# Sixty-four more bytes behind each buffer of a rotating operand: where the tiles lie in SBUF

## The chip, the cores and the metric

The kernel runs on one core of one Trainium2 chip, in one launch. The metric is the device time of that core in microseconds. Before the change three runs took 1132.81, 1133.07 and 1133.88 us, a median of 1133.07 us.

## The reference

Three layers follow each other on 6016 tokens of 256 channels, all in float32.

```
qn, kn = q, k divided by their norms over the tokens          # 6016 x 256 each
a      = softmax(kn.T @ qn / tau)                             # 256 x 256
x      = v @ a                                                # 6016 x 256
h      = relu(x @ w_in)                                       # 6016 x 2048
x      = (h * h) @ w_out                                      # 6016 x 256
xn     = x / sqrt(mean(x * x) + 1e-6) * rms_g
out    = (silu(xn @ w_gate) * (xn @ w_val)) @ w2              # inner width 1536
```

## The kernel before, in words

**Precision.** A float32 product is made from three products of a faster 4-byte type (fp32r). Each operand is split in a high part, a rounded copy, and a low part, the value less the high part. `mm3` (L102 to L105) then issues high by high (L103), high weight by low data (L104) and low weight by high data (L105) into one PSUM bank. Every matmul has 128 rows, 128 columns of weights and up to 512 columns of data, and every one has its own weight load.

**Stages.** The attention part (L449 to L640) runs over q and k once, up to about 62 us. Then the first MLP runs over twelve blocks of tokens, ten of 512 and two of 448 (`mlp1`, L741): for each of 16 slices of the 2048 inner channels `up` issues two `mm3` into one bank, so 6 matmuls, the ScalarE takes relu out of it (tile r, in `o6` or `o7`), the square s goes to `o8` or `o9`, its high part to `sh` (L761 or L764, ScalarE) and its low part to `sl` (L768, VectorE), and `down` (L772) issues 6 matmuls that read `sh` and `sl` into two accumulators. From about 596 us the second MLP (`mlp2`, L959) runs over six pairs of blocks and twelve slices of its inner channels: 21 matmuls at L984 make two blocks' gate and value by seven products of sums and differences; the product of silu and value is split into `sh` (L1047, ScalarE) and `sl` (L1051, VectorE), and again `down` reads both with 12 matmuls, six for each block.

**Order.** The order of the work is written out by hand: `unit` (L704) issues one slice's `up`, its reads, the side work hooked to it and an older slice's `down`. No scheduler or planner looks at an address.

**Tiles.** A pool gives each tag its own place in every partition of SBUF, in the order of the tags' first use, one behind the other. The pool `xp` holds, in this order, `o4`, `o5`, `o10` to `o13`, `o7`, `o9`, five buffers of `sh`, five of `sl`, `o6`, `o8`, two buffers of `ys` (4,096 bytes each; also the split inputs of block 2 and of the second MLP on their way to DRAM, and `x4`), and `xst` (14,336 bytes; in the odd pairs it holds as `xs` three of the second MLP's seven inputs). Behind it lies the small pool `ns`. All other tags are in pools ahead of these. The five `sh` and five `sl` buffers are handed out in turn by `work` (L731):

```
    def work(tag, n):
        return xp.tile([P, NB], F32R, tag=tag, name=tag, bufs=5)[:, :n]
```

NB is 512, so a buffer takes 2,048 bytes of each partition. Every tag in the list is a multiple of 512 bytes long, and each of them starts at 128 mod 512. So does every slice that a matmul of the two MLPs reads, weights too, since those are slices of 128 or 256 four-byte columns.

Of the kernel before, what the change touches and what calls it, by code (L numbers as in the profile page):

```python
# [9 lines left out]
F32R = mybir.dt.float32r  # L10
# [8 lines left out]
P = 128  # L19
NB = 512  # L20
WARM = 8
SIGN = -(2**31)


@with_exitstack
def attn_moe_kernel(ctx: ExitStack, tc, q, k, v, tau, w_in, w_out, w_gate, w_val, w2, rms_g, out):
# [88 lines left out]
    class Call:  # L115
# [27 lines left out]
        def b2(self):  # L143
            gi = self.g.bitcast(I32)
            nc.vector.scalar_tensor_tensor(
                out=gi, in0=self.raw[:, 1::2], scalar=SIGN, in1=gi, op0=ALU.bitwise_and, op1=ALU.bitwise_or
            )
# [301 lines left out]
    with tc.tile_pool(name="qk", bufs=3) as qp:  # L449
# [55 lines left out]
        def warm(count):  # L505
            for _ in range(count):
                nc.tensor.matmul(nk, busy[:, :P], busy, start=True, stop=True)
# [10 lines left out]

        warm(WARM)
        for ci, (j0, nj) in enumerate(chunks):  # L520
# [124 lines left out]
    xp = ctx.enter_context(tc.tile_pool(name="xp", bufs=1, reuse_waits="tile"))  # L645
# [83 lines left out]
            pending.pop(0)()  # L729

    def work(tag, n):  # L731
        return xp.tile([P, NB], F32R, tag=tag, name=tag, bufs=5)[:, :n]

    turns = {"r": 0, "s": 0}

# [5 lines left out]
    def mlp1(b, vt, act_heavy):  # L741
# [4 lines left out]
        def up(f):  # L746
            o = mm()[:, :n]
            fs = slice(f * P, (f + 1) * P)
            for c in range(KC):
                mm3(o, m_h[:, c, fs], m_l[:, c, fs], vt["h"][c], vt["l"][c], c == 0, c == KC - 1)  # L750

            def read(evs):
                r, s = turn("r", n), turn("s", n)
                sh, sl = work("sh", n), work("sl", n)
                sq[f] = sh, sl, s
                nc.scalar.activation(out=r, in_=o, func=AF.Relu)  # L756
                for x in evs:
                    x()
                if act_heavy(f):
                    nc.scalar.activation(out=s, in_=r, func=AF.Square)  # L760
                    nc.scalar.copy(out=sh, in_=s)  # L761
                else:
                    nc.vector.tensor_tensor(out=s, in0=r, in1=r, op=ALU.mult)
                    nc.scalar.activation(out=sh, in_=r, func=AF.Square)  # L764

            def rest():
                sh, sl, s = sq[f]
                nc.vector.tensor_tensor(out=sl, in0=s, in1=f32(sh), op=ALU.subtract)  # L768

            return read, rest  # L770
# [188 lines left out]
    def mlp2(p, ops, after_product, after_group, spare):  # L959
# [17 lines left out]
        def group(f):  # L977
# [67 lines left out]
            def hi(t, x):  # L1045
                parts[t] = work("sh", n), work("sl", n)
                nc.scalar.copy(out=parts[t][0], in_=x)  # L1047
# [181 lines left out]
    n, last_mean = norm_steps(NBLK - 1, ys[NBLK - 1])  # L1229
# [87 lines left out]
```

## Time and profile before

| what | value |
|---|---|
| median of three runs | 1133.07 us |
| profiled execution, from first to last instruction | 1130.9 us |
| TensorE matmul busy | 1118.5 us, 99% |
| ScalarE busy | 764.7 us, 68% |
| VectorE busy | 748.5 us, 66% |
| DMA, mean over the span | 89 GB/s |

The page gives no device time of its own for the profiled execution beside its span. The span is 2.2 us shorter than the median of the runs, and these 2.2 us lie around it, before the first and after the last instruction. A matmul's busy time counts from its start until its modelled end, and matmuls overlap, so 99% busy says that TensorE is hardly ever without a matmul, not how fast they follow each other. For that one reads the distance from one start to the next.

### The profile page before, as it was taken

To read this page: it belongs to the slowest core of one execution; us is meant where nothing else is said; L and a number is where in the kernel's file an instruction comes from. 1 tells how busy PE (TensorE), PEld (TensorE's weight loads), DVE (VectorE), ACT (ScalarE), POOL (GpSimd) and SP (SyncE) were. 2 spreads that over 40 slices of the span, in tenths; PEclk is the share of its full clock that TensorE was granted. 3 is DMA by queue.
4 is the path that set the end of the run, shared out by engine and by line. 5 is a ranking of instruction groups with operands and counts; after the bars stand their busy time and mean duration, and the time that the engine had idled before them with its cause. 6 is when DMAs were issued, how large, how long until landed. Compare 5 with 4: busy or idle time off the path is not lost.

```text
span 1130.9 us, 14479 instructions
## 1 busy us (share of the span) xinstructions
PE 1118.5 (99%) x5222; PEld 943.0 (83%) x5222; DVE 748.5 (66%) x1156; ACT 764.7 (68%) x1382; POOL 72.9 (6%) x99
## 2 busy tenths in 40 slices
PE   8999999999999999999999999999999999999997
PEld 7978888888888888889987888888888888888996
DVE  6998766687777787766556655555655655655655
ACT  7688867677687787776677566556656566556554
POOL 2421110010202020100000000000000000000000
PEclk9999999999999999999999999999999999999999
DMA  9733310231451532320247023202302302202001
GB/s 318 232 112 94 94 38 20 84 121 38 130 159 66 156 139 68 110 101 1 85 149 313 33 103 104 74 1 75 94 1 75 93 1 75 71 16 66 19 19 33
DMA packets 96903, 101.21 MB, mean 89 GB/s; under 512 B 49856, under 2 KB 67520, under 8 KB 96320
## 3 DMA queue, kind: packets, MB, share of 16 engines
q1 hardware_dynamic: 94560, 99.44, 27.7%
q10 hardware_dynamic: 2272, 0.85, 0.3%
q8 instruction: 41, 0.67, 0.3%
q14 instruction: 30, 0.25, 0.1%
HBM read 65.21 MB, written 35.06 MB: 89 GB/s over the span
## 4 chain that ended last, share of the span: by engine, by line
PE 92%; DMA 2%; ACT 2%; DVE 1%; POOL 1%; issue 1%; SPq 1%; DVEq 0%; ACTq 0%
PE mm L984 29%; PE acc L103 13%; PE acc L104 13%; PE acc L105 13%; PE mm L105 7%; PE mm L104 7%; PE mm L103 7%; POOL rows L492 1%; DMA rraw<-in_v_dram 1%; PE mm L683 1%; DMA qraw<-in_k_dram 1%; ACT hl L532 0%; DMA o<-xd 0%; SPq L461 0%; SPq L462 0%
## 5 line engine op out<-in xcount | busy, mean ns | idle before, releaser
L984 PE MATMUL mm<-o,gv 128*128 128x512 f32 (+1 forms) x1152 | 294.5, 387 | 0.7 <-DMA o<-xd 0.6
L984 PEld LDWEIGHTS mm<-o,gv 128*128 128x128 f32 x1152 | 214.9, 188 | 45.6 <-ACT pu L1029 1.1
L768 DVE TENSOR_TENSOR sl<-o,sh 128x512 fp32r<-128x512 f32 (+1 forms) x192 | 134.4, 700 | 104.4 <-ACT sh L761 89.9
L1051 DVE TENSOR_TENSOR sl<-hp,sh 128x512 fp32r<-128x512 f32 (+1 forms) x144 | 98.0, 681 | 143.1 <-ACT sh L1047 142.7
L1012 ACT COPY mm<-mm 128x512 f32<-128x512 f32 (+1 forms) x72 | 40.4, 561 | 183.9 <-PE mm L984 183.9
L756 ACT ACTIVATE o<-mm 128x512 f32<-128x512 f32 (+1 forms) x192 | 112.3, 585 | 69.3 <-PE mm L105 65.8
L103 PE MATMUL acc<-sh,wo_h 128*128 128x512 f32 (+1 forms) x384 | 149.0, 388 | 0.0
L105 PE MATMUL mm<-o,m_l 128*128 128x512 f32 (+1 forms) x384 | 148.2, 386 | 0.4 <-DVE m_l L695 0.4
L105 PE MATMUL acc<-sh,wo_l 128*128 128x512 f32 (+1 forms) x384 | 148.1, 386 | 0.1
L104 PE MATMUL acc<-sl,wo_h 128*128 128x512 f32 (+1 forms) x384 | 148.1, 386 | 0.0
L103 PE MATMUL mm<-o,m_h 128*128 128x512 f32 (+1 forms) x384 | 147.9, 385 | 0.0
L104 PE MATMUL mm<-o,m_h 128*128 128x512 f32 (+1 forms) x384 | 147.9, 385 | 0.0
L103 PE MATMUL acc<-sh,w_h 128*128 128x512 f32 (+1 forms) x284 | 109.5, 386 | 0.0
L105 PE MATMUL acc<-sh,w_l 128*128 128x512 f32 (+1 forms) x284 | 109.5, 385 | 0.0
L104 PE MATMUL acc<-sl,w_h 128*128 128x512 f32 (+1 forms) x284 | 109.5, 385 | 0.0
L1047 ACT CAST sh<-hp 128x512 fp32r<-128x512 f32 (+1 forms) x144 | 89.0, 618 | 2.7 <-DVE hp L1038 1.9
L105 PEld LDWEIGHTS mm<-o,m_l 128*128 128x128 f32 x384 | 72.1, 188 | 14.8 <-DVE m_l L695 1.5
L105 PEld LDWEIGHTS acc<-sh,wo_l 128*128 128x128 f32 x384 | 72.1, 188 | 14.3 <-DVE wo_l L170 0.8
L104 PEld LDWEIGHTS mm<-o,m_h 128*128 128x128 f32 x384 | 72.1, 188 | 13.5
L103 PEld LDWEIGHTS mm<-o,m_h 128*128 128x128 f32 x384 | 72.1, 188 | 13.4
L104 PEld LDWEIGHTS acc<-sl,wo_h 128*128 128x128 f32 x384 | 72.1, 188 | 13.3 <-DVE sl L768 0.4
L103 PEld LDWEIGHTS acc<-sh,wo_h 128*128 128x128 f32 x384 | 72.1, 188 | 13.0 <-ACT wo_h L163 0.2
(153 smaller groups left out, 1767.6 us busy)
## 6 DMA issues: line engine op xcount, KB each, us to landing
xd<-xp SPq DMA_DIRECT2D x70, 256.0 KB, 2.1
o<-xd SPq DMA_DIRECT2D x56, 256.0 KB, 4.6
raw<-in_moe_w_out_dram SPq DMA_DIRECT2D x14, 512.0 KB, 3.7
gv<-gvd SPq DMA_DIRECT2D x4, 1792.0 KB, 14.0
gvd<-gp SPq DMA_DIRECT2D x12, 512.0 KB, 3.2
out_dram<-ot SPq DMA_DIRECT2D x40, 128.0 KB, 2.5
qraw<-in_q_dram SPq DMA_DIRECT2D x13, 384.0 KB, 8.0
qraw<-in_k_dram SPq DMA_DIRECT2D x13, 384.0 KB, 8.1
```

Source lines behind the costliest of these rows:

```text
L103: nc.tensor.matmul(o, wh, xh, start=start, stop=False)
L104: nc.tensor.matmul(o, wh, xl, start=False, stop=False)
L105: nc.tensor.matmul(o, wl, xh, start=False, stop=stop)
L492: nc.gpsimd.tensor_copy(out=rows[:, g], in_=src[:, g])
L683: nc.tensor.matmul(o[m], a_part(t, c, m), w[:, c], start=ts is not last and i == 0, stop=ts is not early and i == len(ts) - 1,)
L756: nc.scalar.activation(out=r, in_=o, func=AF.Relu)
L768: nc.vector.tensor_tensor(out=sl, in0=s, in1=f32(sh), op=ALU.subtract)
L984: nc.tensor.matmul(bank, c[:, hl, a, fs], x, start=start and j == 0, stop=j == 2, skip_group_check=not start)
L1012: cp(out=bu, in_=b0)
L1047: nc.scalar.copy(out=parts[t][0], in_=x)
L1051: dve(out=pl, in0=x, in1=f32(ph), op=ALU.subtract)
```

## The change

The five `sh` buffers are 2,112 bytes apart instead of 2,048. Only their first 512 columns (or 448) are used, as before; the 64 bytes behind them are never read or written.

```
+PAD = 16
     def work(tag, n):
-        return xp.tile([P, NB], F32R, tag=tag, name=tag, bufs=5)[:, :n]
+        width = NB + PAD if tag == "sh" else NB
+        return xp.tile([P, width], F32R, tag=tag, name=tag, bufs=5)[:, :n]
```

The built program has the same instructions on every engine, in the same order and with the same waits. What differs is the addresses (bytes in a partition, and the remainder by 512):

| tiles | before | after |
|---|---|---|
| pools ahead of `xp`; `o4`, `o5`, `o7`, `o9` to `o13` | 128 | 128 |
| `sh`, five buffers | 181,376 and so on, all 128 | 181,376 and so on: 128, 192, 256, 320, 384 |
| `sl`, five buffers | 191,616 and so on, 128 | 191,936 and so on, 448 |
| `o6`, `o8` | 128 | 448 |
| `ys`, two buffers (also `o2` of block 2, `xp`, `x4`) | 128 | 448 |
| `xst`, `xs` | 214,144, 128 | 214,464, 448 |
| `ns`, two buffers of 128 bytes | 128, 256 | 448, 64 |

The tiles of the attention part (`qraw`, `hl`, `rraw`, `ws`, `ws2`) and the buffers of the output (`vraw`, `vt`) stay where they are.

## Rows read from the trace of the kernel before

**Rows 1.** Busy time of each engine, and the granted clock in 40 slices.

```profile
PE 1118.5 (99%) x5222; PEld 943.0 (83%) x5222; DVE 748.5 (66%) x1156; ACT 764.7 (68%) x1382; POOL 72.9 (6%) x99
PEclk9999999999999999999999999999999999999999
```

**Rows 2.** Windows: busy time and (count) of PE, PEld, DVE, ACT, POOL; clock, DMA.

```profile
0.00:70.00 70.00, 65.59 (x468) 59.15 (x469) 57.30 (x78) 51.62 (x73) 22.51 (x44) 0.98 0.78 244
70.00:600.00 530.00, 529.01 (x2410) 444.93 (x2409) 383.26 (x610) 398.81 (x711) 50.38 (x55) 1.00 0.30 96
600.00:1100.00 500.00, 499.94 (x2231) 417.46 (x2231) 292.21 (x444) 301.10 (x573) 0.00 (x0) 1.00 0.20 64
1100.00:1131.00 31.00, 23.99 (x117) 21.44 (x115) 15.70 (x27) 13.21 (x27) 0.00 (x0) 0.94 0.14 30
```

**Rows 3.** Waits of TensorE's matmuls after 70 us: total us, times, longest.

```profile
PE mm L984 <- DMA o<-xd: 0.6, 1, 0.6
PE mm L105 <- DVE m_l L695: 0.4, 1, 0.4
```

**Rows 4.** Chain of waits, 625 to 632 us: start, length, what.

```profile
625.57 2.72 PE mm L984 x12
628.29 0.23 PE acc L103
628.52 0.23 PE acc L104
628.75 0.23 PE acc L105
628.97 1.36 PE mm L984 x6
```

**Rows 5.** Timeline of TensorE in the attention part: start, length, operation.

```profile
25.89 0.28 PE L566 MATMUL acc<-hl 128*128 128x256 f32 x1
...
26.49 0.28 PE L568 MATMUL acc<-hl 128*128 128x256 f32 x1
```

**Rows 6.** Three short windows, columns as in rows 2.

```profile
8.20:9.10 0.90, 0.90 (x6) 0.90 (x6) 0.51 (x1) 0.36 (x1) 0.00 (x0) 0.50 1.08 370
25.80:26.70 0.90, 0.90 (x10) 0.90 (x9) 0.80 (x2) 0.86 (x2) 0.00 (x0) 1.00 1.10 349
625.00:632.00 7.00, 7.00 (x33) 5.79 (x32) 5.55 (x9) 3.95 (x8) 0.00 (x0) 1.00 0.01 2
```

**Rows 7.** Timeline of TensorE in a block of 448 columns.

```profile
559.73 0.36 PE L104 MATMUL acc<-sl,wo_h 128*128 128x448 f32 x1
...
565.60 0.37 PE L103 MATMUL mm<-o,m_h 128*128 128x448 f32 x1
```

**Rows 8.** Tile `sh`: who writes and reads it; ns min/median/max, first and last start.

```profile
L103 PE MATMUL acc<-sh,wo_h x384: 362/389/476, 68.4 to 595.0; 128*128 128x512 f32 x160, 128*128 128x448 f32 x32
L105 PE MATMUL acc<-sh,wo_l x384: 362/389/505, 69.2 to 595.5; 128*128 128x512 f32 x160, 128*128 128x448 f32 x32
L103 PE MATMUL acc<-sh,w_h x284: 362/389/398, 601.2 to 1122.1; 128*128 128x512 f32 x120, 128*128 128x448 f32 x22
```

**Rows 9.** Groups by form: VectorE with two operands; count, busy us, mean ns, idle.

```profile
L1051 DVE TENSOR_TENSOR sl<-hp,sh 128x512 fp32r<-128x512 f32 x120 | 83.1, 692 | 122.2 <-ACT sh L1047 121.9
L1041 DVE TENSOR_TENSOR sg<-mm,pu 128x512 f32<-128x512 f32 x60 | 41.5, 691 | 0.3 <-PE mm L984 0.2
```

**Rows 10.** Line L100 (VectorE, blocks of 448): ns min/median/max, first and last start.

```profile
L100 DVE TENSOR_TENSOR o<-vt,o x4: 618/618/621, 495.7 to 534.5; 128x448 fp32r<-128x448 f32 x4
```

**Rows 11.** Timeline of ScalarE at L99, one block of 512, one of 448.

```profile
446.00 0.60 ACT L99 CAST o<-vt 128x512 fp32r<-128x512 f32 x1
...
448.72 0.61 ACT L99 CAST o<-vt 128x512 fp32r<-128x512 f32 x1
...
494.55 0.55 ACT L99 CAST o<-vt 128x448 fp32r<-128x448 f32 x1
...
497.92 0.56 ACT L99 CAST o<-vt 128x448 fp32r<-128x448 f32 x1
```

**Rows 12.** Waits: who waited for whom, total us, times, longest.

```profile
ACT mm L1012 <- PE mm L984: 183.9, 71, 2.9
DVE sl L1051 <- ACT sh L1047: 142.7, 137, 1.5
ACT xp L897 <- DMA xd<-xp: 19.9, 19, 2.0
```

**Rows 13.** DMA issues: count, KB each, median us from issue to landing.

```profile
xd<-xp SPq DMA_DIRECT2D x70, 256.0 KB, 2.1
o<-xd SPq DMA_DIRECT2D x56, 256.0 KB, 4.6
xs<-xd SPq DMA_DIRECT2D x6, 512.0 KB, 5.5
```

**Rows 14.** Timeline of TensorE at the start.

```profile
8.21 0.41 PE L568 MATMUL acc<-hl 128*128 128x256 f32 x1
...
9.06 0.41 PE L558 MATMUL mm<-hl 128*128 128x256 f32 x1
```

## The prediction

> **What bounds the kernel now.** I read the busy lines of the page first: TensorE has a matmul in flight for 99% of the span, VectorE and ScalarE work for two thirds of it [rows 1]. The windows then say where: from 70 to 1100 us TensorE is busy 529.01 + 499.94 = 1028.95 of 1030 us, at a granted clock of 1.00, its upper level of 2.4 GHz; only the first 70 us and the last 31 us have gaps, of 4.4 and 7.0 us [rows 2]. The waits agree: after 70 us matmuls waited twice, 1.0 us in all [rows 3].
>
> A busy engine may still run slowly, so the third thing to read is the distance from start to start. In the chain, twelve matmuls of 512 columns take 2.72 us, 226.7 ns each; six take 1.36 us, again 226.7; the three that read `sh` and `sl` take 0.68 us from 628.29 to 628.97, 226.7 [rows 4]. Matmuls that read `sh`, `sl` and other tiles follow each other at one pace. With 256 columns five distances make 0.60 us, 120 ns each [rows 5], at the same clock [rows 6]. The second 256 columns therefore cost 226.7 - 120 = 106.7 ns, 0.417 ns a column, and 13.3 ns per matmul are left that don't depend on its length. With 448 columns this line gives 13.3 + 448 x 0.417 = 200.0 ns; the trace has 29 distances in 565.60 - 559.73 = 5.87 us, 202.4 ns, 2.4 above the line [rows 7]. So the time is the number of matmuls times their pace, plus a start and an end. Only what changes the pace, or makes TensorE wait, is worth anything.
>
> **The change part by part.** Nothing is removed or added, and no instruction is put elsewhere. What can be costed is only whether an access takes another time because its place has another remainder by 512. I take the engines in turn.
>
> *TensorE.* How many matmuls read moved data? The `sh` view counts 384 matmuls at L103 and 384 at L105 in the first MLP, 284 at either line in the second [rows 8], and the last step (L1074) adds 8: 1344 that read `sh`, four for each of 336 uses of a buffer. One buffer in five stays at 128, which leaves 268 uses, 1072 matmuls. `sl` is read by half as many as `sh`, 672, all moved. `xs` holds three inputs in three of six pairs: 3 x 12 slices x 3 products x 3 = 324. `x4` gives 12 x 3 = 36; `o6` and `o8`, the high parts of two inputs, 6 x 12 x 2 x 2 = 288; block 2's inputs, 16 x 6 = 96. Together 2488 of 5222. No weight moves.
>
> What does one cost? The trace has no large matmul that reads data at another remainder, so I bound it. From below, the 13.3 ns that don't depend on the length could go: 2488 x 13.3 ns = 33.1 us less. From above, the nearest row in which a matmul costs more than the line gives is that of 448 columns, 2.4 ns: 2488 x 2.4 ns = 6.0 us more. I take nothing. In 625 to 632 us VectorE works 5.55 and ScalarE 3.95 of 7 us, in 25.8 to 26.7 us both nearly always [rows 6], all on tiles that begin at the same remainder as TensorE's, and the pace is the same to the last digit in each piece of the chain [rows 4]. A collision with other engines over equal remainders would come and go with them. What is left, a fixed rest per matmul, nothing in the trace ties to an address.
>
> *VectorE and ScalarE.* Equal remainders cost nothing that could be won: L1051 reads two SBUF tiles and writes a third, all at 128 mod 512, in 692 ns, while L1041, with one of its operands in PSUM, takes 691 [rows 9]. Other remainders do occur in the trace: in the blocks of 448 columns the second half of `vt` begins 1,792 bytes behind the first, at 384 mod 512. L100 reads it beside an operand at 128 and writes to 128; of its four instructions two are such, and the four lie between 618 and 621 ns [rows 10]. ScalarE's L99 takes 0.55 us at 128 and 0.56 at 384, but in a block of 512, where both halves are at 128, also 0.60 and 0.61 [rows 11], so this hundredth belongs to the second half and not to its place. I take 0, with 3 ns either way. What covers it: in the second MLP ScalarE waits 183.9 us for TensorE and VectorE 142.7 us for ScalarE [rows 12], and from 70 to 600 us they are busy 398.81 and 383.26 of 530 us [rows 2]. Were that cover gone, 3 ns on each of some 600 moved instructions of one engine would be 1.8 us.
>
> *DMA.* Moves of `ys` to DRAM land after 2.1 us, loads of `xs` after 5.5 us [rows 13]. ScalarE waits 19.9 us for the former [rows 12], beside a TensorE that goes on; TensorE itself waited 0.6 us for loads [rows 3]. Here a rule speaks against the change. The Trainium skill, "DMA: Bandwidth & Descriptors", section "How a descriptor splits into AXI transactions", says that a transfer which starts off a 256-byte boundary also pays for the bytes from that boundary to its start. By it a row of 2,048 bytes starting at 192 instead of 128 past the boundary would cost 70 beats instead of 68, an estimate of 3%: some 0.06 us on each 2.1 us, and 0.02 us on the one wait that TensorE feels. No run here shows it yet; the sum leaves it out.
>
> *Start and end.* The attention part's tiles, the output's buffers and the loads that both wait for stay where they are, so the 4.4 and 7.0 us of gaps stay.
>
> The sum is 0: a span of 1130.9 us, and with the 2.2 us that lie between it and the median of the runs 1133.1 us.
>
> **The rivals.**
>
> *Slower: a read of 2,048 bytes from an odd multiple of 64 bytes costs TensorE more.* The place is the two MLPs' matmuls on data at remainders 192, 320 and 448: two `sh` buffers (134 uses, 536 matmuls) and the other 1416 moved ones, 1952 in all. The price is 2.4 ns, as for 448 columns: 4.7 us, 1137.8 us; if the two other `sh` buffers paid too, 6.0 us, 1139.1 us. It decides from 1.2 ns on, when it passes 2.3 us. For it: reads of 1,024 and 2,048 bytes lie on the line, the read of 1,792 bytes, which ends in the middle of a 512-byte piece, lies above it, so pieces of that size may matter to the pace. Against it: in the blocks of 448 everything starts at 128, so those 2.4 ns may belong to the length alone.
>
> *Faster: the fixed 13.3 ns are a collision between TensorE's own two reads.* Data and weights both begin at 128 mod 512 now; moved data would pass the weights. The price is up to 33.1 us, 1100.0 us, or 1116.6 us if half of it goes. For it: at the lower clock level, 1.2 GHz (0.50 in [rows 6]), 256 columns take 0.85 us / 4 = 212 ns [rows 14], 0.83 ns a column with no rest at all, so the rest isn't a number of the array's own cycles; something that keeps its own time shows through at full clock. Against it: a collision should depend on where the two streams stand to each other, and the rest is the same for 256 and 512 columns, for weights from `gv` (L984), `w2_h` and `w2_l` (L103, L105). The Trainium skill, "TensorE: Matmul & The Clock Gate", gives 2.5 ns over the columns in "Back-to-back issue gap", 215.8 ns for 512, and two separate read ports in "Step-by-step: what each phase is for". The trace disagrees with the first by 10.9 ns; reaching it on all moved matmuls would be an estimate of 27 us less, 1106 us, and by the second rule no collision exists to remove.
>
> *The other engines set the pace.* For VectorE or ScalarE to bind, the busier one would need a third more work than its 398.81 of 530 us; 3 ns in 600 is half a percent. Or they get faster and TensorE's waits go: at most the 1.0 us of [rows 3].
>
> *The change does nothing because nothing moved:* excluded, the tiles' places are in the built program.
>
> **How the numbers follow.** No change 0.80; the slower rival 0.11; the faster one 0.09, most of it small parts of its price. Runs of this kernel tell a change from none at about 0.2%, 2.3 us. My range starts at 1133.1 - 1.0 (all waits of rows 3) - 2.3 = 1129.8 us and ends at 1137.8 us, the slower rival's price; it leaves out the rest of the faster one and the dearer form of the slower one, under 2 in 10. Faster by over 0.2%: 0.09; within 0.2%: 0.80; slower by over 0.2%: 0.11.
>
> **What would show it.** In the profile after, twelve matmuls at L984 should still take 2.72 us, three at L103 to L105 0.68 us, and 29 distances of 448 columns 5.87 us. L1051 should stay at 692 ns and L768 should not spread by buffer. If the pace of L103 to L105 differs from that of matmuls on `o0` to `o5`, which have not moved, a rival is right, and its sign is the sign of the change. If the pace holds and the time still moves, it must be in TensorE's waits, and the prediction failed at the cover of the other engines.

## The result: 17 us slower, all of it in the pace of the matmuls

The changed kernel takes 1149.89 us (median of four, 1149.69 to 1149.93), the kernel before 1132.94 us: a ratio of 1.0149, with a 95% interval of 1.0135 to 1.0163. The forecast was no change, with a range that ended at 1137.8 us.

The busy line and the windows after, columns as in [rows 1, 2]:

```profile
PE 1134.5 (99%) x5222; PEld 942.5 (82%) x5222; DVE 748.6 (65%) x1156; ACT 767.8 (67%) x1382; POOL 72.1 (6%) x99
```

```profile
70.00:600.00 530.00, 529.50 (x2379) 439.63 (x2378) 379.84 (x605) 393.70 (x699) 51.18 (x55) 1.00 0.28 90
1117.00:1148.00 31.00, 24.19 (x119) 21.67 (x117) 15.98 (x27) 13.23 (x27) 0.00 (x0) 0.95 0.14 30
```

VectorE's and ScalarE's busy time is the same within half a percent. TensorE is as full as before and the clock is 1.00, but in the same 530 us it starts 2379 matmuls instead of 2410. The last 31 us hardly differ. TensorE's waits after 70 us are no longer than in [rows 3]:

```profile
PE mm L986 <- ACT pu L1022: 0.5, 1, 0.5
PE mm L106 <- DVE m_l L696: 0.3, 1, 0.3
PE acc L106 <- DVE wo_l L171: 0.2, 1, 0.2
```

So it is the distance from start to start, the pace. The chain of waits after, to hold against [rows 4] (L984 is now L986, L103 to L105 are L104 to L106), first from the second MLP, then from the first:

```profile
634.79 2.78 PE mm L986 x12
637.57 0.23 PE acc L104
637.80 0.23 PE acc L105
638.04 0.23 PE acc L106
638.27 1.39 PE mm L986 x6
```

```profile
302.01 0.23 PE mm L104
...
303.39 0.23 PE acc L104
```

Twelve matmuls take 2.78 us instead of 2.72, 231.7 ns each; the three that read `sh` and `sl` 0.70 us instead of 0.68, 233.3. The six from 302.01 to 303.39 read `o10` to `o13`, which have not moved, and take 230 ns instead of 226.7. With 448 columns nothing has changed: 29 distances in 5.88 us, 202.8 ns, as in [rows 7]. Nor has the attention part, whose tiles didn't move: five distances of 256 columns in 0.60 us, as in [rows 5]. The first two lines below are from the block of 448 columns, the other two from the attention part.

```profile
568.17 0.36 PE L104 MATMUL acc<-sh,wo_h 128*128 128x448 f32 x1
...
574.05 0.37 PE L106 MATMUL mm<-o,m_l 128*128 128x448 f32 x1
```

```profile
26.03 0.28 PE L567 MATMUL acc<-hl 128*128 128x256 f32 x1
...
26.63 0.28 PE L569 MATMUL acc<-hl 128*128 128x256 f32 x1
```

The 3902 matmuls of 512 columns behind the attention part carry the whole: 16.95 us / 3902 = 4.3 ns each. The start times in the two traces bear this out: without the few distances over 260 ns the mean of all 512-column distances is 227.0 ns before and 231.4 after, that of 448 columns 202.8 both times.

### The profile page after: what moved, and what is told of

The parts are those of the page before. It is cut to its first block, busy times and chain, and to the rows that moved or that the text cites. A ratio compares the mean times of both kernels' runs of the same rounds, so it can differ in the third digit from the quotient of the medians.

```text
span 1148.1 us, 14479 instructions
## 1 busy us (share of the span) xinstructions
PE 1134.5 (99%) x5222; PEld 942.5 (82%) x5222; DVE 748.6 (65%) x1156; ACT 767.8 (67%) x1382; POOL 72.1 (6%) x99
## 4 chain that ended last, share of the span: by engine, by line
PE 92%; ACT 2%; DVE 2%; DMA 1%; POOL 1%; issue 1%; SPq 0%; DVEq 0%; ACTq 0%
PE mm L986 30%; PE acc L104 13%; PE acc L106 13%; PE acc L105 13%; PE mm L104 7%; PE mm L105 7%; PE mm L106 7%; POOL rows L493 1%; DMA rraw<-in_v_dram 1%; PE mm L684 1%; ACT hl L533 1%; DMA qraw<-in_k_dram 0%; DVE hl L534 0%; DVE dg L142 0%; DVE ws L518 0%
## 5 line engine op out<-in xcount | busy, mean ns | idle before, releaser
L986 PE MATMUL mm<-o,gv 128*128 128x512 f32 (+1 forms) x1152 | 298.4, 390 | 0.5 <-ACT pu L1022 0.5
L986 PEld LDWEIGHTS mm<-o,gv 128*128 128x128 f32 x1152 | 215.4, 188 | 49.6 <-ACT pu L1022 0.9
L1053 DVE TENSOR_TENSOR sl<-hp,sh 128x512 fp32r<-128x512 f32 (+1 forms) x144 | 98.1, 681 | 145.6 <-ACT sh L1049 145.2
L104 PE MATMUL acc<-sh,wo_h 128*128 128x512 f32 (+1 forms) x384 | 150.7, 392 | 0.0
L104 PE MATMUL mm<-o,m_h 128*128 128x512 f32 (+1 forms) x384 | 150.0, 391 | 0.0
L106 PE MATMUL acc<-sh,wo_l 128*128 128x512 f32 (+1 forms) x384 | 149.4, 389 | 0.3 <-DVE wo_l L171 0.2
L105 PE MATMUL acc<-sl,wo_h 128*128 128x512 f32 (+1 forms) x384 | 149.3, 389 | 0.0
L106 PE MATMUL mm<-o,m_l 128*128 128x512 f32 (+1 forms) x384 | 149.0, 388 | 0.3 <-DVE m_l L696 0.3
L105 PE MATMUL mm<-o,m_h 128*128 128x512 f32 (+1 forms) x384 | 149.2, 388 | 0.0
L106 PE MATMUL acc<-sh,w_l 128*128 128x512 f32 (+1 forms) x284 | 110.9, 391 | 0.0
L105 PE MATMUL acc<-sl,w_h 128*128 128x512 f32 (+1 forms) x284 | 110.6, 389 | 0.0
L104 PE MATMUL acc<-sh,w_h 128*128 128x512 f32 (+1 forms) x284 | 110.4, 389 | 0.0
L106 PEld LDWEIGHTS mm<-o,m_l 128*128 128x128 f32 x384 | 72.1, 188 | 16.7 <-DVE m_l L696 1.4
L106 PEld LDWEIGHTS acc<-sh,wo_l 128*128 128x128 f32 x384 | 72.1, 188 | 16.2 <-DVE wo_l L171 1.1
L104 PEld LDWEIGHTS acc<-sh,wo_h 128*128 128x128 f32 x384 | 72.2, 188 | 14.6 <-ACT wo_h L164 0.2
L105 PEld LDWEIGHTS mm<-o,m_h 128*128 128x128 f32 x384 | 72.1, 188 | 14.6
L104 PEld LDWEIGHTS mm<-o,m_h 128*128 128x128 f32 x384 | 72.1, 188 | 14.5
L105 PEld LDWEIGHTS acc<-sl,wo_h 128*128 128x128 f32 x384 | 72.2, 188 | 13.8
```

Of the source, the lines that this page charges most:

```text
L104: nc.tensor.matmul(o, wh, xh, start=start, stop=False)
L105: nc.tensor.matmul(o, wh, xl, start=False, stop=False)
L106: nc.tensor.matmul(o, wl, xh, start=False, stop=stop)
L986: nc.tensor.matmul(bank, c[:, hl, a, fs], x, start=start and j == 0, stop=j == 2, skip_group_check=not start)
L1053: dve(out=pl, in0=x, in1=f32(ph), op=ALU.subtract)
```

## The experiments

Three programs run matmuls alone: 200 of each sequence, each with its own weight load, the output in a bank that nobody reads, no other engine beside them. Two tiles, W for weights and D for data, begin at the same remainder by 512; a sequence says how many bytes further data and weights begin, in turn. The other programs are the kernel before with padding elsewhere.

**e1: matmuls alone, which sequence is slow.**

```
W = wp.tile([P, 2048], F32R); D = wp.tile([P, 4096], F32R)
a = (i % 6) * 128 + wrem[i % len(wrem)] // 4          # six weight slices in turn
s = starts[i % len(starts)] // 4
mm(out=bank[i % 8][:, :n], lhsT=W[:, a : a + 128], rhs=D[:, s : s + n], start=True, stop=True)
```

> A program of matmuls alone (200 for each of 27 sequences, one bank after the other, six weight slices in turn, nothing else running; it leaves out the whole computation and writes q to the output). It takes three theories apart. SWITCH: a matmul is slower when its data begin at another remainder by 512 than the data of the matmul ahead of it; the changed kernel has 1920 such places among its matmuls of 512 columns and is 17 us longer, 8.9 ns each. Then data at one place, whichever, and 0/512 keep 226.7 ns, and alternating 0/64, 0/128, 0/320 take some 235.6 ns; if only the remainder by 256 or 128 counts, 0/256 or 0/128 stay at 226.7. WEIGHTS: a matmul is slower when its data lie at another remainder than its weights; there are 2044 of these, 8.3 ns each. Then data at one place 64 or 256 bytes off the weights take 235.0 ns, an alternation of 0 and 64 only 230.9, and weights and data both at 64 take 226.7. OTHERS: ScalarE, VectorE or DMA collide with the moved reads; then every sequence here takes 226.7 ns. For 448 columns SWITCH has no reason for the 2.4 ns above the line unless it is the end of a read and not its start that the next one is held against; then 0/256 with 448 columns falls to 200.0 ns.

The chain of waits shows one piece of 200 matmuls for each line. In order: data at the weights' remainder (L47), 64 bytes off it (L50), 256 off (L53), alternating 0/512 (L56), 0/16 (L59), 0/64 (L62), 0/128 (L65), 0/256 (L68), 0/320 (L71), 0/320/0 like the three products (L74), six and six (L77), 448 columns (L92), 448 columns alternating 0/256 (L95), weights alternating 0/64 with data at one place (L107), and data and weights both 64 further (L110).

```profile
70.99 45.33 PE b L47 x200
116.33 45.79 PE b L50 x200
162.12 45.34 PE b L53 x200
207.47 45.33 PE b L56 x200
252.80 46.32 PE b L59 x200
299.12 46.34 PE b L62 x200
345.46 46.01 PE b L65 x200
391.47 45.37 PE b L68 x200
436.84 46.18 PE b L71 x200
483.02 46.40 PE b L74 x200
529.42 46.22 PE b L77 x200
...
760.76 41.33 PE b L92 x200
802.09 41.33 PE b L95 x200
...
945.42 46.50 PE b L107 x200
991.92 45.36 PE b L110 x200
```

The pace of the kernel before comes back, 45.33 us / 200 = 226.7 ns, and so does that of the change: 232.0 ns for the three products' pattern and 231.1 for six and six, 4.4 to 5.3 ns over it, where the changed kernel has 4.3. OTHERS falls: no other engine is needed. With 512 columns only the remainder by 256 counts here, 0/256 and 256 off the weights cost nothing. SWITCH has the sign right and too high a price (231.7 against 235.6 ns for 0/64), and it has no room for the 2.3 ns of data that all lie 64 off the weights, nor for weights that alternate while data stay, 232.5 ns. WEIGHTS asks 8.3 ns for the former. SWITCH's idea for 448 columns, that the end of a read counts, falls as well: alternating 0/256 leaves them at 206.7 ns. That value itself is a riddle, since the kernel before takes 202.4 ns at equal remainders [rows 7]; no run shows why. What counts involves both places, that of the data and that of the weights: apart by 64 bytes they cost 2.3 ns, both 64 further nothing (L110, 226.8). A matmul of bf16 shows none of it when its data alternate (data at 0, L116, and 0/64, L119); bf16 weights were not moved:

```profile
1082.69 10.74 PE b L116 x49
...
1125.85 10.74 PE b L119 x49
```

**e2: all data 64 bytes further.** One pad ahead of the pool of `o0` to `o3`, one that brings the weights behind it back to 128, one ahead of all other data.

```
+    vp.tile([P, 16], F32, tag="pad0", name="pad0")
...
+    mp.tile([P, 112], F32, tag="pad1", name="pad1")
+    xp.tile([P, 16], F32, tag="pad2", name="pad2")
```

> All data of the two MLPs lie 64 bytes further, at 192 mod 512, and all weights stay at 128. SWITCH: no two successive data reads begin at different remainders, so no change, 1133 us. WEIGHTS: all 3902 matmuls of 512 columns read data and weights at different remainders, 8.3 ns each, 32 us more, 1165 us. OTHERS: the tiles that ScalarE, VectorE and TensorE share keep one remainder among themselves, no change.

It takes 1138.98 us against 1132.72 us for the kernel before, run alongside: 1.0059, from 1.0044 to 1.0074. Both theories fail: nothing switches, yet it is 6.3 us slower, and that is a fifth of what WEIGHTS wants. The matmuls alone have it: 228.9 ns at 64 off the weights, and here twelve take 2.75 us, 229.2 ns:

```profile
636.38 2.75 PE mm L987 x12
```

On 3902 matmuls that would make 8 to 9 us. About 2 us of it come back in the blocks of 448 columns, which also lie 64 bytes off the weights here: their mean distance is 200.1 ns in this trace, 202.8 in that of the kernel before.

**e3 and e4: the two halves of the change.**

```
+        width = NB + 16 if tag == "sh" else NB                        # e3, and in work, once:
+            pads.append(xp.tile([P, 48], F32, tag="pad", name="pad"))  # ahead of the first sl
```

```
+            pads.append(xp.tile([P, 80], F32, tag="pad", name="pad"))  # e4: alone, ahead of the first sl
```

> The five sh buffers as in the change (128, 192, 256, 320, 384), and 192 bytes of padding behind them that bring sl and all later tiles back to 128. SWITCH: 1425 places with a change of remainder, 8.9 ns each, 12.7 us more, 1145.6 us. WEIGHTS: 896 matmuls with data off the weights' remainder, 8.3 ns each, 7.4 us more, 1140.4 us.

> sh stays at 128; 320 bytes of padding move sl, o6, o8, ys and xst to 448, as in the change. SWITCH: 1511 places, 13.4 us more, 1146.4 us. WEIGHTS: 1148 matmuls, 9.5 us more, 1142.5 us. The two parts of the change by SWITCH add up to more than the whole (26.1 against 17 us), because a switch from sh to sl counts in both.

The rotation of `sh` alone takes 1142.92 us (1.0094, 1.0077 to 1.0111), the moved tail alone 1146.96 us (1.0128, 1.0113 to 1.0143). SWITCH asked for 1145.6 and 1146.4, WEIGHTS for 1140.4 and 1142.5; SWITCH has the order and the second value, neither has both. Either half costs most of the whole, 10.2 and 14.2 us, and they don't add up (24.4 against 17 us); that a stream already out of step loses little more by a second cause would explain it, and was not tested by itself.

**e5: matmuls alone, other distances and shorter weights.** As e1.

> A second program of matmuls alone (200 for each of 27 sequences; it leaves out the whole computation and writes q to the output). In the first one data 64 bytes off the weights cost 228.9 ns, 256 bytes off 226.7, and alternating data or alternating weights 230 to 234. TWO READS: each matmul's data are read while the next one's weights are, and the two hinder each other unless they keep step; only their addresses by 256 count. Then weights alternating 0/256 stay at 226.7 and 0/128 go to about 230; a fixed distance other than 64 gives paces between 226.7 and 232, perhaps one below 226.7, since nothing says that distance 0 is the best; and weights of 64 or 32 columns, a shorter second read, lower both the fixed 13.3 ns (to about 6.7 and 3.3 if it goes by their number) and the cost of alternating. OWN REST: the 13.3 ns belong to the 4-byte data read itself and only the alternation is a collision; then 64 and 32 weight columns keep 226.7 ns, and no distance is below it. For 256 columns, alternating 0/64 costs by TWO READS as much per matmul as with 512, about 5 ns (125 instead of 120 ns).

Fixed distances from the weights of 4 (L47), 16 (L53), 64 (L62) and 128 bytes (L74); 448 columns at 64 (L89) and 128 (L92); weights of 64 (L101) and 32 columns (L107); weights alternating 0/256 (L110) and 0/128 (L113); 256 columns with data alternating 0/64 (L122):

```profile
71.08 47.33 PE b L47 x200
...
165.07 46.33 PE b L53 x200
...
304.73 45.79 PE b L62 x200
...
489.64 46.66 PE b L74 x200
...
723.13 40.01 PE b L89 x200
763.13 40.79 PE b L92 x200
...
885.26 46.00 PE b L101 x200
...
977.48 46.34 PE b L107 x200
1023.81 45.37 PE b L110 x200
1069.18 46.67 PE b L113 x200
...
1185.18 23.62 PE b L122 x200
```

With 512 columns the remainder of the weights is better than each of fourteen other distances tried, which cost 228.9 to 236.7 ns, 128 bytes and 4 bytes too. With 448 columns it is the worst of the four tried, 206.7 ns (e1) against 200.0 at 64 bytes, 204 at 128 and 202 at 192. Weights of 64 columns give 230 ns, of 32 columns 231.7, more than 226.7: both theories of the fixed rest fall, OWN REST, since the weights' shape changes the pace, and the version by which the rest goes by their number of columns. And 256 columns alternating 0/64 take 118.1 ns, less than the 120 of one place, where 125 were expected. The cost follows a pattern that length, shape and distance all enter; it is no sum of prices per matmul. That the two reads hinder each other is how I read it; the runs show only that the places of both enter.

**e6: the tail moved by 256 instead of 320 bytes.** As e4 with 64 columns of padding.

> As the run with the tail alone moved, but by 256 bytes instead of 320: sl, o6, o8, ys and xst at 384 mod 512, sh and the rest at 128. If addresses count by 256 (the sequences 0/256 and 256 off the weights kept 226.7 ns), no change, 1132.7 us. If they count by 512 in the kernel (other engines' reads and writes among it), the 1511 switches of remainder cost as with 320 bytes, 14 us, 1147 us.

The ratio is 0.9999 (0.9990 to 1.0009). The same tiles moved as in e4, but by a distance that keeps the remainder by 256: the 14 us are gone, and twelve matmuls of 512 columns take what they took before.

```profile
633.87 2.72 PE mm L988 x12
```

With 448 columns the remainder by 256 isn't the whole story. In the last pair of the second MLP, the only one with 448 columns, twelve matmuls take 2.43 us in the kernel before (202.5 ns) and 2.48 us in e6 (206.7 ns, the value of e1). First before, then e6:

```profile
1085.37 2.43 PE mm L984 x12
```

```profile
1086.85 2.48 PE mm L988 x12
```

One execution of each is traced, so whether the 256 bytes did this or it differs from run to run stays open.

**e7: matmuls alone, which two reads.** As e1.

> A third program of matmuls alone (200 for each of 22 sequences; it leaves out the whole computation and writes q to the output). It asks which two reads hinder each other. NEXT: a matmul's data and the weights that are loaded meanwhile for the next matmul. Then data 0/64 with weights 64/0, equal at every moment when both are read, keep 226.7 ns, and data 0/64 with weights 0/64 take about 233. OWN: a matmul's data and its own weights; then it is the other way round. STREAM: a change between successive data reads alone; then both take about 231.7 ns as data 0/64 did. A further sequence (20 at one place, 20 at 320 bytes further) shows how many matmuls a change is felt for: one or two by STREAM with the others at 226.7, all 20 of the half with unequal places by NEXT or OWN. 20 and 20 at 0 and 256 keep 226.7 by all. Lengths of 496, 504 and 510 columns, no multiples of 128, leave the line as 480 did (216.7 against 213.3).

Data 0/64 with a matmul's own weights equal (L47) and with the next one's equal (L50), data 0/128 with its own weights equal (L53), 20 and 20 at 0 and 320 (L62), at 0 and 256 (L65); 448 columns at 64 (L71); data 0/192 (L89); 496 (L101) and 504 columns (L104):

```profile
71.16 46.33 PE b L47 x200
117.48 46.32 PE b L50 x200
163.80 45.67 PE b L53 x200
...
300.84 45.69 PE b L62 x200
346.53 45.35 PE b L65 x200
...
437.53 40.01 PE b L71 x200
...
685.53 45.34 PE b L89 x200
...
870.57 44.00 PE b L101 x200
914.57 45.33 PE b L104 x200
```

Neither pairing restores the pace, 231.7 and 231.6 ns, so NEXT and OWN fall, as simple pairings. With 0/128 equal own weights win back half, 228.4 ns instead of the 230.0 of weights at one place (e1). STREAM, one or two slow matmuls after a change, falls by the 20 and 20: L62 would have to be nearer to 226.7 than its 228.5 ns. Half its matmuls lie 64 off by 256, and in the trace the distances after a change to them run 237, 235, 232, 231 ns and then stay between 225 and 233. Back at 0 they run 230, 231, 231, 228 ns before the pace is 226 or 227 again. There are two costs: one of a fixed wrong distance, 2.3 ns at 64 bytes, and one of each change. Over four matmuls the change into the wrong distance costs 935 - 4 x 229 = 19 ns beyond that, the change back 920 - 4 x 226.7 = 13 ns. One alternation, 0/192, costs nothing, which was not expected. Of the lengths, 504 columns left the line, as expected, and cost what 512 cost; 496 did not leave it.

**e8: what the pace of 448 columns offers.** The operands of the two short blocks begin 64 bytes into their places, which have 256 bytes to spare.

```
+    def shifted(n):
+        return slice(16, 16 + n) if n < NB else slice(0, n)
-        return xp.tile([P, NB], F32R, tag=tag, name=tag, bufs=5)[:, :n]
+        return xp.tile([P, NB], F32R, tag=tag, name=tag, bufs=5)[:, shifted(n)]
```

and so for the inputs in `v_tiles` and `fetch`.

> The kernel before, with the operands of the two blocks of 448 columns begun 64 bytes into their 2,048-byte places; nothing else moves. Matmuls alone took 206.7 ns with 448 columns at the weights' remainder, 200.0 at 64 bytes off it. In the kernel before they take 202.4. TWO READS: 200.0 in the kernel too, 2.4 ns for 780 matmuls, 1.9 us less, 1130.9 us (0.998 of before). A cost of any place other than the weights' (as with 512 columns, 228.9 for 226.7): 2.2 ns more for 780, 1.7 us more, 1134.5 us.

It takes 1130.62 us, 0.9981 of the kernel before (0.9972 to 0.9990): faster than both kernels, by 2.3 us where 1.9 were expected. Its timeline has 29 distances of 448 columns in 5.79 us, 199.7 ns against 202.4 in [rows 7]:

```profile
560.12 0.36 PE L106 MATMUL mm<-o,m_h 128*128 128x448 f32 x1
...
565.91 0.36 PE L108 MATMUL acc<-sh,wo_l 128*128 128x448 f32 x1
```

## Why the prediction was wrong

- **The bound was right, the step after it wrong.** Time is the number of matmuls times their pace, plus start and end: the whole difference lies in the pace, and waits, start, end, VectorE, ScalarE and DMA came out as forecast. L1053 takes 693 ns where [rows 9] have 692, L101 618 to 620 as in [rows 10].
- **The step that failed is the price of a moved read on TensorE, "I take nothing".** It was argued from a pace that was the same in every piece of the chain. But all those pieces had one layout by address, data and weights at equal remainders, so an even pace couldn't tell a rest that no address touches from one that sits at its best address. The matmuls alone show the second: 226.7 ns at distance 0, 228.9 to 236.7 at fourteen others.
- **The bound from above was too low and of the wrong form.** 2.4 ns on each of 2488 moved reads, 6.0 us, stood against 17. The runs show 4.3 ns on all 3902 matmuls of 512 columns, because matmuls on unmoved data pay beside their neighbours: in the first MLP those on the blocks' inputs, block 2 left out, take 231.2 ns on average instead of 226.8. That unmoved data pay after a change back is what e7's four distances show. So the sign that the prediction named, a pace of `sh` and `sl` that differs from that of unmoved tiles, hardly appears.
- **The slower rival had engine and sign, but not the rule.** It read the 448 columns, above the line with everything at 128, as a sign that places matter to the pace. They do: e8 took those nanoseconds away. But its reason, a read that ends inside a 512-byte piece, failed in e1 (0/256 with 448 columns), so the hint was in part luck. Its odd multiples of 64 were wrong, since fixed distances of 16 and 128 bytes cost more than 64, and its price was too small.
- **The line was drawn through the two points that it was to explain.** That 256 and 512 columns lie on it and share a rest of 13.3 ns, which the prediction used for the one rival and against the other, follows from how it was drawn. A third length was needed: in e1 384 columns take 173.3 ns, on the line, and 480 take 216.7, off it.
- **The faster rival came nearest to the cause, TensorE's own two reads, with the sign reversed.** With 512 columns equal remainders are not a collision but the best of the distances tried. The Trainium skill, "TensorE: Matmul & The Clock Gate", section "Step-by-step: what each phase is for", has the weights on a read port of their own that takes nothing from the running matmul; it was held against this rival. With 4-byte operands e1 speaks against it: alternating the weights' place alone, data unmoved, takes 232.5 instead of 226.7 ns. The bf16 sequences of e1 don't, their pieces of 49 keep 10.74 us, but there only the data moved.
- **The DMA rule's 3% is not seen.** The moves from `ys` land in 2.1 us as in [rows 13], but 0.06 us would hardly show in a time given to 0.1 us. The loads of `xs`, which moved too, land in 5.4 us where it was 5.5; 3% would have been 0.2 us more.

What stays open is why the distance matters as it does: which part of the fixed 13.3 ns is the two reads, why alternating 0/192 is free and 0/128 is not, why 448 columns want another distance than 512, and why they take 202.4 ns in the kernel and 206.7 alone. The runs show that the places of both reads take part and that no other engine is needed.

## What to carry to other kernels

Where fp32r matmuls of 512 columns follow each other without a gap, as here, the distance between data and weights by 256 bytes, and changes of either place from one matmul to the next, are part of their pace: 2 to 10 ns in 227. Pad by multiples of 256 bytes, as e6 did, keep all operands of a length at one remainder, and measure the best distance for each length with matmuls alone before laying out tiles. A pace that is even in a trace says nothing of layouts that the trace does not have.

## What the runs showed of the hardware that was not expected

- 512 columns of fp32r take 226.7 ns with data and weights at one remainder by 256, up to 236.7 ns at 4 bytes' distance (e1, e5). bf16 shows nothing of it with data alternating 0/64 (e1).
- 448 columns alone are slowest, of four distances, where 512 are fastest: 206.7 ns at equal remainders, 200.0 at 64 bytes (e1, e5). In the kernel before equal remainders gave 202.4.
- 504 columns take as long as 512 (226.7 ns), 496 take 220.0 ns (e7).
- Halving the weights' columns to 64 made a stream slower, 230.0 ns instead of 226.7 (e5).
